# A fused attention and feed-forward block: where attention's steps are let into the matmul stream

## The chip, the cores and the metric

The kernel runs on one core of a Trainium2 chip. A core has a matrix engine (PE, TensorE), a vector engine (DVE), a scalar engine (ACT), a general engine (POOL, GpSimd) and a synchronising engine (SP); each works through its own queue in the order in which the program gave it the instructions, and waits there for semaphores of the others. DMAs are issued from the queues of SP, ACT and POOL. The metric is the device time of one execution in microseconds. Before the change the median of three runs is 1107.38 us (1107.1 to 1107.52).

## The reference

All tensors are float32; S = 2048 positions, D = 576, F = 4608, 32 heads of 18.

```python
x = A_x
xn = layernorm(x)                                  # no scale, no shift
q, k, v = split(xn @ wqkv)                         # 32 heads of 18
idx = pos[:, None] - 2 * arange(8)[None, :]        # 8 keys: this position, 2, 4, ... 14 before it
logits = einsum("bhsd,bhswd->bhsw", q, k[idx]) * 18 ** -0.5   # idx < 0: -1e9
o = einsum("bhsw,bhswd->bhsd", softmax(logits), v[idx])
attn = o @ wo
h = relu(xn @ w1 + b1); ffn = (h * h) @ w2 + b2
out = x + attn + ffn
```

The result is returned as [1, 2048, 576].

## The kernel before

**Tiling.** The positions are four blocks b of 512 (`TB`), worked on in two pairs, s = 0 (blocks 0, 1) and s = 1 (blocks 2, 3). float32 precision is had from two parts of every operand: a high part (an ACT copy into a type that PE takes fast) and a remainder (a DVE subtraction); each product is high by high, high by remainder and remainder by high, 128x128 weights against 512 positions. FFN1 of two blocks and two tiles of hidden units is one 2x2 block product, done with seven products instead of eight (slots T1, T3, B11, T2, B22, B21, T4; the sums of X are S1 to S3). What does not fit the 128-row grid (the last 64 rows of D) is a "left" product; in s = 1, from pair 2 on, it is replaced by one more matmul per product against a *stack* (`ST`, `LW`).

**Phases, in PE's order.** Layer norm and QKV of block 0; QKV of block 1 (`q0`); phase A of s = 0: 18 FFN1 pairs of block 0 and 1 with FFN2 of block 0 interleaved (`ffn_pair`, `work`); FFN2 of block 1 (`phase_b0`), while DVE and ACT normalise blocks 2 and 3; QKV of blocks 2 and 3 as four *halves* (k, half) of 14 quad steps each (`quads`, `quad_step`), the last two steps of which stand inside pair 0 of s = 1; phase A of s = 1; FFN2 of block 3 (`phase_b1`).

**An FFN1 pair** (line 605 on). PE: B11 into bank `ba`, T1 into `bc`, FFN2 work, T2 into `bb`, work, T3 into `bb`, B21 into `ba`, work, B22 into `bc`, T4 into `bb`, work. Between products ACT and DVE must free the banks: ACT copies `bb` to `u[:, 0]` after T2 (line 691) and to `u[:, 1]` after T3 (line 723), DVE adds `bc` to it (`r1[:, 1]`, line 725, recorded at the helper line 108), which is what B22 into `bc` waits for; later DVE adds `r0[:, 1]`, ACT does the `relu`s and squares. `splits` makes the high parts and remainders of the next weights: `w2_hi` (509), `w2_lo`, `w1_hi` (477), `left_weight_hi` (595). In pair 1 of s = 1 the stacks are built too: `stack_hi` on ACT, `stack_lo` on DVE, from the left rows `LR["a"]`.

**Attention runs beside PE.** Keys, values and queries are written by the QKV rows to memory (`kvq`) through a staging tile `st` of four places and loaded back per block and head group by POOL. `attention(b, g)` is a generator of 18 steps: four times a product of q and k (`qk`) and a reduction, a maximum with a subtraction that yields "exp", the exponential (ACT, line 396) with its sum, reciprocal and product, and four times a product with v (`pv`) and three halving sums. `statistics(b)` has four steps. `side(k, exp)` takes k steps of whatever is at the head of the queue; with `exp=False` it stops in front of an exponential. The places at which `side` is called, and with which k, are written out by hand: at the head of a pair, in its third product, at its end, in a table of quad steps, in the chunks of the output projection, between the tiles of FFN2. A step's K and V are loaded as soon as one of three `kv` tiles is given back. `complete(b)` runs whatever is still due before a block's attention output is gathered (`regroup`).

**QKV rows of blocks 2 and 3.** Each half produces eight rows (`row`, line 1047): an ACT copy of a bank into a place of `st` (line 1050), for every second one a DVE sum on top, and a store of 216 KB to `kvq` (line 1054) issued by ACT or SP. A place is used again four rows later. The tile `w1r` has two slots, used in turn for raw weights, left rows, stacks and left weights.

Of the kernel before, what the change touches and what calls it, by code (L numbers as in the profile page):

```python
# [8 lines left out]
F32 = mybir.dt.float32  # L9
# [7 lines left out]
P = 128  # L17
# [4 lines left out]
NJ = TB // P  # L22
# [6 lines left out]
QW = 3 * CG  # L29
# [10 lines left out]
T1, T3, B11, T2, B22, B21, LEFT, T4 = range(8)  # L40
# [5 lines left out]
def block_kernel(ctx: ExitStack, tc: tile.TileContext, x, xt, wqkv, wo, w1, b1, w2, b2, w1l, out):  # L46
# [3 lines left out]
    sb = ctx.enter_context(tc.tile_pool(name="sb", bufs=1))  # L50
# [24 lines left out]
    half = const.tile([P, 1], F32, name="half")  # L75
# [31 lines left out]
    def tt(out, a, b, op):  # L107
        return nc.vector.tensor_tensor(out=out, in0=a, in1=b, op=op)  # L108
# [204 lines left out]
    qp, stage = {}, {}  # L313
# [105 lines left out]
    current = [None, None, None]  # L419

    def side(k, exp=True):

        while k > 0:
            if current[0] is None:
                if not queue or queue[0][0] not in landed:
                    return k
                name, make = queue.pop(0)
                current[:] = [make(), None, name]
            if current[1] == "exp" and not exp:
                return k  # L430
            try:
                current[1] = next(current[0])
                k -= 1
            except StopIteration:
                current[0] = None
        return 0
# [38 lines left out]
    def w1_hi(n, k):  # L475
        w1s[n, k] = mt.tile([P, 2, 4, 2 * P], F32R, name="w1s", bufs=3)
        nc.scalar.activation(w1s[n, k][:, 0], raw1[n][:, 4 * k:4 * k + 4], AF.Copy)  # L477
# [33 lines left out]
    def w2_lo():  # L511
        i = los[0]
        los[0] += 1
        if i >= len(stream):
            return
        w = w2s[stream[i]]
        tt(w[:, DE:], raw2.pop(i)[:, :D], w[:, :D].bitcast(F32), ALU.subtract)
        load_w2(i + 3)
# [25 lines left out]
    ST, LW, LR = {}, {}, {}  # L544
# [16 lines left out]
    def stack_hi(to, v):  # L561
        nc.scalar.activation(to, v, AF.Copy)

    def stack_lo(to, v):
        rows = slice(L, 2 * L)
        tt(to[rows], v[rows], to[rows].bitcast(F32), ALU.subtract)
# [27 lines left out]
    def left_weight_hi(p):  # L594
        nc.scalar.activation(LW[p % 2], LR["w"], AF.Copy)

    def left_weight_lo(p):
        rows = slice(2 * L, P)
        tt(LW[p % 2][rows], LR["w"][rows], LW[p % 2][rows].bitcast(F32), ALU.subtract)
        load_left_weights(p + 1)  # L600
# [4 lines left out]
    def ffn_pair(s, p, work, first=False):  # L605
        b0, b1 = 2 * s, 2 * s + 1
        n = s * NP + p
# [73 lines left out]
            stack_hi(LR["st"][:, 0:2], LR["a"][:, 0:2])  # L681
            stack_hi(ST[T4], LR["a"][:, 3])
        if not first:
            side(1 if p == 1 else 3 if s else 2 + p % 2, s == 1)
        work(0)
        product(bb, T2, ss(2))
        own_w2 = first and s == 1
# [10 lines left out]
        def splits():  # L698
            if not own_w2:
                w2_lo()  # L700
            if not last and not s:
                w1_hi(n + 1, 0)
            if ready:
                left_weight_hi(p + 1)
            if s and p == 1:
                stack_lo(LR["st"][:, 0:2], LR["a"][:, 0:2])
                stack_lo(ST[T4], LR["a"][:, 3])
                stack_hi(ST[T1], LR["s"][:, 0])
            if not own_w2:
                w2_hi()  # L710
            if not last and not s:
                w1_lo(n + 1, 0)
            if ready:
                left_weight_lo(p + 1)
            if not own_w2:
                w2_lo()

        if not first:
            splits()
# [3 lines left out]
        nc.scalar.activation(u[:, 1], bb, AF.Copy)  # L723
        r0, r1 = four(), four()
        tt(r1[:, 1], bc, u[:, 1], ALU.add)
        if first:
            splits()
        if not last and s:
# [298 lines left out]
    rows_out = [0]  # L1027

    def quad_step(k, s, j, i):
        b0, b1, gs = 2, 3, (2 * k, 2 * k + 1)  # L1030
        a, b, c, u = [bank(n)[:, :QW] if opened is None else opened for n, opened in
                      zip((*QKV_BANKS[i], i), quad_banks[i])]
        quad_banks[i] = [a, b, c, u]
        js = slice(j * P, (j + 1) * P)

        def product(to, name, v, start=False):
            mm = [(v(0, n), ws[name][0][:, n]) for n in range(2)]
            for n in range(2):
                mm += [(v(0, n), ws[name][1][:, n]), (v(1, n), ws[name][0][:, n])]
            for n, (l, r) in enumerate(mm):  # L1040
                nc.tensor.matmul(to, l[:, js], r, start=start and n == 0, stop=n == len(mm) - 1, skip_group_check=True)  # L1041

        def left(to, f, v):
            for n in range(2):
                nc.tensor.matmul(to, v[:, js], ws[LEFT, f][:, n], start=False, stop=n == 1, skip_group_check=True)  # L1045

        def row(n, f, x, y=None):
            st = stage[0][:, rows_out[0] % NJ]
            rows_out[0] += 1
            nc.scalar.activation(st, x, AF.Copy)  # L1050
            if y is not None:
                tt(st, y, st, ALU.add)
            to = kvq[gs[f]][:, PAD + n * TB:PAD + (n + 1) * TB].rearrange("i (p j) c -> p j i c", j=NJ)[:, j]
            (nc.sync if y is not None else nc.scalar).dma_start(to, st.rearrange("p (i c) -> p i c", c=CG))

        ss = lambda n: lambda h, q: SS[n][:, h, q]
        if s == 1:
            product(a, B11, lambda h, q: X[b0][:, h, q], start=True)
            nc.scalar.activation(b, a, AF.Copy)
        if s == 2:  # L1060
            product(c, T1, ss(1), start=True)
        if s == 3:
            product(b, T2, ss(2))
            nc.scalar.activation(u, b, AF.Copy)
        if s == 4:
            left(c, 1, x4[b1])
            product(b, T3, ss(3))
            row(b1, 1, b, c)
        if s == 5:
            product(a, B21, lambda h, q: X[b0][:, h, 2 + q])  # L1070
            left(a, 0, x4[b0])
            row(b0, 0, a)
        if s == 6:
            product(c, B22, lambda h, q: X[b1][:, h, q])
            left(c, 1, x4["d"])
            row(b0, 1, c, u)
        if s == 7:
            product(b, T4, lambda h, q: X[b1][:, h, 2 + q])
            left(b, 0, x4[b1])
            row(b1, 0, b)  # L1080
# [3 lines left out]
    def phase_b0():  # L1084
# [41 lines left out]
        def hook(k, half, s, i):  # L1126
# [9 lines left out]
            if half and not k:  # L1136
# [32 lines left out]
                if (s, i) == (6, 1):  # L1169
# [3 lines left out]
                    for g in (0, 1):  # L1173
                        offer(2, g)
            if half and k:
                if (s, i) == (2, 1):
                    w1_again(NP, 0, nc.sync)
                if (s, i) == (5, 1):
                    complete(1)
                if (s, i) == (4, 1):  # L1180
                    w1_again(NP, 1, nc.sync)
# [5 lines left out]
        def quads(k, half, some):  # L1187
            for n in some:
                s, i = steps[n]
                quad_step(k, s, 2 * half + i, i)  # L1190
                if n in ((2, 3, 4, 8, 10, 12), (3, 6, 10, 12), range(1, 13), (3, 6, 8, 10))[2 * k + half]:
                    side(1)
                hook(k, half, s, i)

# [426 lines left out]
```

## Time and profile before

| | |
|---|---|
| median of three runs | 1107.38 us |
| profiled execution | 1107.93 us |
| its span, first to last instruction | 1106.2 us |
| PE busy / weight loads busy | 1096.8 / 925.2 us |
| DVE busy | 912.0 us |
| ACT busy | 575.0 us |
| POOL busy | 115.4 us |
| moved by DMA | 287.83 MB, mean 260 GB/s |
| granted clock of TensorE | 1.000 |

The page gives busy times by engine and by groups of instructions. A row of the waits reads: engine, line, what it waited for, us in total, how often, longest. A row of the order of time reads: start, duration, engine, line, operation, output<-input, shape, count, and in brackets the idle time before it with what ended it. Matmuls are pipelined: a 128x512 matmul is recorded with about 389 ns, and the next one starts before it ends, so the distance of starts is what to compare. SPq, ACTq, POOLq are the queues' own instructions, DMA issues among them.

### The profile page before, as it was taken

The numbers are of one execution on the slowest core, as the hardware profiler recorded it, in microseconds if no ns is written. First come the engines' busy times: TensorE is split into PE (matmuls) and PEld (weight loads), VectorE is DVE, ScalarE is ACT, GpSimd is POOL, SyncE is SP. The second block draws the span as 40 slices with busy tenths as digits, with TensorE's granted clock in tenths as the row PEclk, the third lists the DMA queues.
The fourth block names the chain that finished last, engine by engine and source line by source line (L and its number), as shares of the span: only waits on it lengthen the run. The fifth ranks groups of instructions, "written<-read, shape, count | busy, mean of one in ns | idle before, by whom it ended". The sixth has DMA issues, their size and how long they took to land.

```text
span 1106.2 us, 13892 instructions
## 1 busy us (share of the span) xinstructions
PE 1096.8 (99%) x4950; PEld 925.2 (84%) x4950; DVE 912.0 (82%) x1223; ACT 575.0 (52%) x809; POOL 115.4 (10%) x219
## 2 busy tenths in 40 slices
PE   9999999999999999999999999999999999999998
PEld 7998888888888888888899887888888888888887
DVE  7696979897996979999979488978988789899654
ACT  5435666556566654455344355555555555533342
POOL 4000101020020100100010200202102021000100
PEclk9999999999999999999999999999999999999999
DMA  8956987889699686866755887768686785866752
GB/s 297 329 177 234 333 309 255 296 214 372 229 244 392 220 357 214 311 247 226 259 164 169 309 263 300 259 260 308 238 315 240 267 314 205 316 208 205 280 193 81
DMA packets 100279, 287.83 MB, mean 260 GB/s; under 512 B 13288, under 2 KB 41712, under 8 KB 85488
## 3 DMA queue, kind: packets, MB, share of 16 engines
q1 hardware_dynamic: 65280, 188.15, 49.1%
q0 software_dynamic: 10544, 52.14, 12.9%
q10 hardware_dynamic: 24384, 46.64, 12.6%
q8 instruction: 39, 0.64, 0.2%
q14 instruction: 32, 0.26, 0.1%
HBM read 205.14 MB, written 81.74 MB: 259 GB/s over the span
## 4 chain that ended last, share of the span: by engine, by line
PE 89%; DVE 5%; DMA 3%; ACT 1%; issue 1%; ACTq 0%; POOL 0%; DVEq 0%; POOLq 0%; SPq 0%
PE p L536 46%; PE p L629 31%; PE p L1041 5%; PE p L635 3%; DMA kvq<-st 2%; PE p L338 1%; PE p L1401 1%; PE p L1045 1%; DVE pr L108 1%; DMA kv<-kvq 1%; DVE lg L387 1%; DVE w1r L108 1%; DVE r L108 0%; PE p L1318 0%; DVE h L108 0%
## 5 line engine op out<-in xcount | busy, mean ns | idle before, releaser
L536 PE MATMUL p<-h,w2s 128*128 128x512 f32 x2066 | 491.4, 389 | 0.1
L536 PEld LDWEIGHTS p<-h,w2s 128*128 128x128 f32 x2066 | 387.5, 188 | 81.5 <-ACT h L642 0.6
L629 PE MATMUL p<-X,w1s 128*128 128x512 f32 x864 | 219.7, 389 | 1.2 <-DVE r L108 0.9
L629 PEld LDWEIGHTS p<-X,w1s 128*128 128x128 f32 x864 | 162.0, 188 | 35.6 <-DVE r L108 1.3
L509 ACT ACTIVATE w2s<-w2r 128x640 fp32r<-128x640 f32 x164 | 120.2, 735 | 116.1 <-PE p L536 87.6
L629 PE MATMUL p<-S,w1s 128*128 128x512 f32 x648 | 164.8, 390 | 1.5 <-ACT r L691 1.5
L108 DVE TENSOR_TENSOR w2s<-w2r,w2s 128x576 fp32r<-128x576 f32 x164 | 123.4, 753 | 40.6 <-ACT w2s L509 39.8
L629 PEld LDWEIGHTS p<-S,w1s 128*128 128x128 f32 x648 | 121.4, 188 | 27.4 <-ACT r L691 2.3
L415 POOL DMA_DIRECT2D o<-q x128 | 69.2, 605 | 584.8 <-DVE q L108 582.8
L638 ACT ACTIVATE r<-r,b1t 128x512 f32<-128x512 f32 x72 | 52.0, 723 | 126.9 <-DVE r L108 125.2
L387 DVE TENSOR_REDUCE lg<-pr 128x64 f32<-128x1152 f32 x64 | 86.5, 1352 | 1.5
L108 DVE TENSOR_TENSOR pr<-lg,kv 128x1152 f32<-128x1152 f32 x64 | 86.7, 1354 | 1.3
L108 DVE TENSOR_TENSOR pr<-q,kv 128x1152 f32<-128x1152 f32 x64 | 86.6, 1353 | 0.8
L108 DVE TENSOR_TENSOR pr<-pr 128x576 f32<-128x576 f32 (+1 forms) x128 | 77.5, 605 | 3.2
L646 ACT ACTIVATE r<-r 128x1024 f32<-128x1024 f32 x72 | 76.1, 1057 | 1.2
L108 DVE TENSOR_TENSOR h<-r,h 128x1024 fp32r<-128x1024 f32 (+3 forms) x46 | 51.8, 1136 | 27.0 <-ACT r L646 18.8
L108 DVE TENSOR_TENSOR r<-p,r 128x512 f32<-128x512 f32 (+1 forms) x77 | 52.9, 688 | 20.3 <-PE p L629 9.8
L108 DVE TENSOR_TENSOR w1s<-w1r,w1s 128x1024 fp32r<-128x1024 f32 (+1 forms) x42 | 50.3, 1198 | 16.5 <-ACT w1s L477 16.4
L691 ACT ACTIVATE r<-p 128x512 f32<-128x512 f32 x36 | 21.5, 597 | 70.9 <-PE p L629 70.5
L638 ACT ACTIVATE r<-p,b1t 128x512 f32<-128x512 f32 x72 | 48.3, 672 | 0.0
L108 DVE TENSOR_TENSOR h<-h 128x1024 fp32r<-128x1024 f32 x36 | 43.9, 1220 | 4.8 <-ACT h L938 4.6
L536 PE MATMUL p<-w1s,w2s 128*128 128x512 f32 x195 | 44.7, 389 | 0.0
(193 smaller groups left out, 1174.2 us busy)
## 6 DMA issues: line engine op xcount, KB each, us to landing
w2r<-in_w SPq DMA_DIRECT2D x144, 320.0 KB, 3.4
kv<-kvq POOLq DMA_DIRECT2D x29, 1296.0 KB, 9.4
w<-w1s SPq DMA_DIRECT2D x36, 1024.0 KB, 8.4
w1s<-w ACTq DMA_DIRECT2D x34, 1024.0 KB, 7.3
h<-r SPq DMA_DIRECT2D x36, 512.0 KB, 6.3
h<-h SPq DMA_DIRECT2D x36, 512.0 KB, 4.2
w1r<-in_w SPq DMA_DIRECT2D x18, 640.0 KB, 7.7
kvq<-st ACTq DMA_DIRECT2D x48, 216.0 KB, 3.2
```

Of the source, the lines that this page charges most:

```text
L108: return nc.vector.tensor_tensor(out=out, in0=a, in1=b, op=op)
L338: nc.tensor.matmul(p[:, :QW], l, r, start=k == 0, stop=k == len(mm) - 1)
L387: nc.vector.tensor_reduce(out=lg[:, j * HG:(j + 1) * HG].rearrange("p a w -> p w a"), in_=pr.rearrange("p w (a d) -> p w a d", d=DH), axis ...
L415: nc.gpsimd.dma_start(rows[:, i], q[i * L:(i + 1) * L, :, a:z])
L509: nc.scalar.activation(w2s[stream[i]][:, :DE], raw2[i], AF.Copy)
L536: nc.tensor.matmul(yp[b][c], v, a, start=c not in yb[b], stop=c in last and c not in [o[0] for o in ops[i + 1:]], skip_group_check=True)
L629: nc.tensor.matmul(to, l, r, start=start and i == 0, stop=i == len(mm) - 1, skip_group_check=True)
L635: nc.tensor.matmul(to, weight(LEFT, k, f), v, start=False, stop=k == 1, skip_group_check=True)
L638: nc.scalar.activation(to, a, AF.Relu, bias=b1t[:, f:f + 1])
L646: nc.scalar.activation(r, r, AF.Square)
L691: nc.scalar.activation(u[:, 0], bb, AF.Copy)
L1041: nc.tensor.matmul(to, l[:, js], r, start=start and n == 0, stop=n == len(mm) - 1, skip_group_check=True)
```

## The change

There are four edits.

- `side` remembers at its start whether the generator stood at "exp" already when the call began (`pending`). If so, the exponential may be the first step of a call even with `exp=False`. An exponential reached within the call still stops it.
- The call at the head of a pair always has `exp=False`, and its k is changed. For s = 0 from 2 in even and 3 in odd pairs to 2, and 3 in every fourth (3, 7, 11, 15); for s = 1 from 3 to 2 in even and 3 in odd pairs. Pair 1 keeps 1. The table of the last QKV half calls `side` after steps 3 and 6 instead of 3, 6, 8 and 10.
- In pair 1 of s = 1 the two first `stack_lo` calls move from `splits` to a place behind the sum `r1[:, 1]`.
- In the last QKV half a second staging tile is opened in a slot of `w1r`; the first four rows of that half go to the first tile, the other four to the second.

```diff
     def side(k, exp=True):
 
+        pending = current[1] == "exp"
         while k > 0:
...
-            if current[1] == "exp" and not exp:
+            if current[1] == "exp" and not exp and not pending:
                 return k
+            pending = False
             try:
                 current[1] = next(current[0])
                 k -= 1
...
         if not first:
-            side(1 if p == 1 else 3 if s else 2 + p % 2, s == 1)
+            side(1 if p == 1 else 2 + (p % 4 == 3 if not s else p % 2), False)
         work(0)
...
             if s and p == 1:
-                stack_lo(LR["st"][:, 0:2], LR["a"][:, 0:2])
-                stack_lo(ST[T4], LR["a"][:, 3])
                 stack_hi(ST[T1], LR["s"][:, 0])
...
         tt(r1[:, 1], bc, u[:, 1], ALU.add)
+        if s and p == 1:
+            stack_lo(LR["st"][:, 0:2], LR["a"][:, 0:2])
+            stack_lo(ST[T4], LR["a"][:, 3])
         if first:
             splits()
...
         def row(n, f, x, y=None):
-            st = stage[0][:, rows_out[0] % NJ]
+            st = stage[rows_out[0] // NJ % len(stage)][:, rows_out[0] % NJ]
...
             if half and k:
+                if (s, i) == (1, 0):
+                    stage[1] = sb.tile([P, NJ, QW], F32, name="w1r", bufs=2)
                 if (s, i) == (2, 1):
                     w1_again(NP, 0, nc.sync)
...
-                if n in ((2, 3, 4, 8, 10, 12), (3, 6, 10, 12), range(1, 13), (3, 6, 8, 10))[2 * k + half]:
+                if n in ((2, 3, 4, 8, 10, 12), (3, 6, 10, 12), range(1, 13), (3, 6))[2 * k + half]:
                     side(1)
```

## The prediction

> **What bounds the kernel now.** I read the page's first part, then the waits of PE alone, then the order of time around each wait.
>
> ```profile
> span 1106.2 us, 13892 instructions
> PE 1096.8 (99%) x4950; PEld 925.2 (84%) x4950; DVE 912.0 (82%) x1223; ACT 575.0 (52%) x809; POOL 115.4 (10%) x219
> ```
>
> ```profile
> PE p L1318 <- DVE lg L1311: 2.1, 1, 2.1
> PE p L629 <- ACT r L691: 1.5, 2, 0.8
> PE p L629 <- DVE r L108: 0.9, 1, 0.9
> ```
>
> PE is the bound. The first wait is the kernel's start, which the change does not touch; the other two rows are three single stalls in FFN1's second half (line 629 is `product`). The most that an edit of ACT's, DVE's or SP's order can bring is the sum of these stalls. The order of time of PE shows them:
>
> ```profile
> 625.89 0.55 PE L1045 MATMUL p<-r,x 128*128 128x432 f32 x2
> 626.28 1.52 PE L629 MATMUL p<-S,w1s 128*128 128x512 f32 x6
> ...
> 628.82 0.55 PE L1045 MATMUL p<-r,x4d 128*128 128x432 f32 x2
> 630.21 1.65 PE L629 MATMUL p<-S,w1s 128*128 128x512 f32 x6 [0.85 <-ACT r L691]
> 631.70 0.70 PE L635 MATMUL p<-x,w1s 128*128 128x512 f32 x2
> ...
> 658.58 1.75 PE L536 MATMUL p<-h,w2s 128*128 128x512 f32 x7
> 660.17 1.52 PE L629 MATMUL p<-S,w1s 128*128 128x512 f32 x6
> 661.53 1.52 PE L629 MATMUL p<-X,w1s 128*128 128x512 f32 x6
> ...
> 663.34 1.75 PE L536 MATMUL p<-h,w2s 128*128 128x512 f32 x7
> 666.02 1.65 PE L629 MATMUL p<-X,w1s 128*128 128x512 f32 x6 [0.93 <-DVE r L108]
> 667.51 0.62 PE L635 MATMUL p<-x4d,w1s 128*128 128x512 f32 x2
> ...
> 677.71 1.75 PE L536 MATMUL p<-h,w2s 128*128 128x512 f32 x7
> 680.16 1.66 PE L629 MATMUL p<-S,w1s 128*128 128x512 f32 x6 [0.70 <-ACT r L691]
> ```
>
> Matmuls overlap, so starts are compared, not idle time. Undisturbed, two matmuls of line 1045 are followed after 0.39 (625.89 to 626.28), a block of seven after 1.59 (658.58 to 660.17), six of `product` after 1.36 (660.17 to 661.53). Stall 1: 630.21 - 628.82 - 0.39 = 1.00 us; stall 2: 666.02 - 663.34 - 1.59 = 1.09; stall 3: 680.16 - 677.71 - 1.59 = 0.86. The first six matmuls after a stall take 1.49 instead of 1.36 (630.21 to 631.70, 666.02 to 667.51), 0.13 more each. Together 1.00 + 1.09 + 0.86 + 3 x 0.13 = 3.34 us, 0.30% of the time. That is the ceiling of this change.
>
> A measurement of this kernel can tell about 0.2% (2.2 us) from no change; so nearly the whole ceiling must be reached for a visible gain.
>
> **The change part by part.**
>
> ```profile
> 628.59 0.53 ACT L1050 ACTIVATE st<-p 128x432 f32<-128x432 f32 x1 [4.46 <-DMA kvq<-st]
> ...
> 678.58 0.42 ACT L396 ACTIVATE lg<-lg 128x256 f32<-128x256 f32 x1 [1.74 <-DVE lg L108]
> ...
> 679.53 0.58 ACT L691 ACTIVATE r<-p 128x512 f32<-128x512 f32 x1
> ```
>
> ```profile
> 662.64 1.82 DVE L108 TENSOR_TENSOR w1r<-w1r 32x1024 fp32r<-32x1024 f32 x2
> 664.48 0.76 DVE L108 TENSOR_TENSOR w2s<-w2r,w2s 128x576 fp32r<-128x576 f32 x1
> 665.27 0.69 DVE L108 TENSOR_TENSOR r<-p,r 128x512 f32<-128x512 f32 x1
> ...
> 684.18 0.68 DVE L108 TENSOR_TENSOR r<-p,r 128x512 f32<-128x512 f32 x1
> ```
>
> *Eight places (stall 1).* Row 7 of the last QKV half goes into a place of `st` whose earlier content is still on its way to memory; ACT stands 4.46 us (628.59) with the bank copy of line 691 behind it, for which PE stops. With rows 5 to 8 in a second tile none of them waits for a store of its own half, and the copy follows T2 at once: -1.13 (1.00 and its restart). The new tile takes a slot of `w1r`, whose two raw weight tiles were read for the last time at the end of the second half; `open_stacks` takes the slot over in pair 1, behind the five chunks of the output projection, when its stores have long landed. So the slot costs nothing. But one thing stands right behind this stall:
>
> ```profile
> PEld p L635 <- DMA w1s<-w: 0.2, 1, 0.2
> w1s<-w SPq DMA_DIRECT2D x1, 1024.0 KB, 11.1
> 616.93 0.77 POOL L360 DMA_DIRECT2D kv<-kvq  x1
> kv<-kvq POOLq DMA_DIRECT2D x29, 1296.0 KB, 9.4
> kv<-o POOLq DMA_DIRECT2D x1, 768.0 KB, 8.9
> ```
>
> The weights of line 635, issued on SP behind a row store, land after 11.1 us; PE took them at 631.70 with 0.2 of waiting. Without stall 1 it wants them 1.0 earlier. They are slow because POOL's V load (616.93, 1296 KB) and the output gather behind it (768 KB and a smaller part) run at the same time: about 3.1 MB in 11.1 us, 0.28 MB/us. By the count of steps below, V load and gather go out some 12 us earlier, while a K load of 1296 KB, which before waited for a step in pair 1, comes forward to about 612. All three should be nearly through when the weights are issued: if only the 768 KB are out of the way, the weights land 2.7 us earlier (an estimate from these rows), and 1.0 is needed. I take the cost as nothing; its bounds are nothing and the whole 1.13.
>
> *Remainders after the sum (stall 2).* The two `stack_lo` (1.82 us) stood ahead of the sum `r1` at 665.27 for which PE waits. Now the second `w2s` remainder can start at 662.64 (0.76) and the sum at 663.4, done at 664.1, while PE arrives at 663.34 + 1.59 = 664.93. Margin 0.8: -1.09 and the restart, -1.22. The 1.82 is only moved, to 664.1 until 665.9, where DVE stood at the end of the sum before (665.27 + 0.69). Behind it wait `left_weight_hi` on ACT, whose tile reuses the slot of `LR["a"]`, and through it DVE's own weight remainder; both come after the `relu` of the sum, which is now 1.8 earlier, so the wait for the pair is covered. The stacks are first multiplied in pair 2.
>
> *Exponential (stall 3).* Pair 2 takes max, exponential and a product at its head; ACT waits 1.74 for DVE's subtraction, and line 691 comes only at 679.53. By the count below, attention (2,0) now has its exponential in pair 0, between FFN2's chunks, and pair 2 begins with a sum and a product. Line 691 then runs as soon as T2 is done: -0.86 and the restart, -0.99. What is late next: `r1` of pair 2.
>
> ```profile
> 685.05 1.54 PE L629 MATMUL p<-X,w1s 128*128 128x512 f32 x6
> ```
>
> Before, `r1` ended at 684.86, 0.19 before PE wanted the bank (685.05). PE now comes 0.86 + 1.09 = 1.95 earlier; DVE gains 1.09 with PE, and max, exponential and product give way to sum and product, which saves the maximum and DVE's wait for ACT, an estimated 1.0. The margin stays about 0.2: I take +0.1, bounds 0 and +0.5.
>
> *The number of steps.* Counted by hand through `side`. FFN1's first half (s = 0): pairs 2 to 17 asked for 8 x 2 + 8 x 3 = 40 leading steps and all calls together lost 15 steps standing at "exp"; now they ask for 12 x 2 + 4 x 3 = 36 and lose 3, at the ends of pairs 2, 5 and 15. So 40 - 15 = 25 become 33: eight more are done, and all that follows comes eight steps earlier. Attention (1,0), which ended in the last half, ends at the sixth step of the half before. In s = 1 pairs 2 to 17 ask for 40 instead of 48, and with the losses at "exp" and the two steps taken from the last half the end of all attention moves from tile 16 to tile 20 of the last phase, ten tiles before its output is wanted (tile 30). Every K and V load is still issued at least a pair ahead of its step, in program order on the same queues; no step should wait for data.
>
> Eight added steps in the first half: DVE must hide them.
>
> ```profile
> 153.30 1.23 DVE L108 TENSOR_TENSOR w1s<-w1r,w1s 128x1024 fp32r<-128x1024 f32 x1 [2.86 <-ACT w1s L477]
> ...
> 155.75 0.69 DVE L108 TENSOR_TENSOR r<-p,r 128x512 f32<-128x512 f32 x1 [0.46 <-ACT r L723]
> ```
>
> ```profile
> 158.32 1.52 PE L629 MATMUL p<-X,w1s 128*128 128x512 f32 x6
> ```
>
> This is pair 3, whose head was empty and gets three steps: exponential, product and sum, at most 1.35 + 2.90 = 4.3 us by the rows below. DVE idles 2.86 + 0.46 ahead of `r1`, and `r1` ends 158.32 - 155.75 - 0.69 = 1.88 before PE needs its bank: 5.2 of room. I cost these steps at nothing; the cover left is 0.9.
>
> The shifted steps in the QKV halves are the one place without room:
>
> ```profile
> 590.69 1.35 DVE L108 TENSOR_TENSOR pr<-q,kv 128x1152 f32<-128x1152 f32 x1
> ...
> 598.80 0.60 DVE L108 TENSOR_TENSOR st<-p,st 128x432 f32<-128x432 f32 x1
> 599.31 1.35 DVE L108 TENSOR_TENSOR pr<-lg,kv 128x1152 f32<-128x1152 f32 x1
> 600.69 1.25 DVE L108 TENSOR_TENSOR pr<-pr 128x576 f32<-128x576 f32 x2
> ...
> 602.21 0.60 DVE L108 TENSOR_TENSOR st<-p,st 128x432 f32<-128x432 f32 x1
> ```
>
> ```profile
> 600.61 1.33 PE L1041 MATMUL p<-h,X 128*128 128x432 f32 x6
> ```
>
> In the third half DVE is behind. Six steps stand ahead of row (4,0)'s sum: 8.11 us (590.69 to 598.80); PE writes that bank again at 600.61, 1.21 after the sum's end. Now these six are three pairs of product and sums, 2.90 each (599.31 to 602.21): 8.70, +0.59. The half before ends on a sum instead of a reduction (+0.2) and has the exponential behind ACT's row copy: DVE's wait there lies between 0 and the 1.74 that the engines cost each other at 678.58; I take 0.5, nearer to nothing, since both queues come there at about the same time. So 0.59 + 0.2 + 0.5 = 1.3 against 1.21: a new stall of 0.1 plus 0.13 of restart, and 0.2 at the next such row. Cost +0.4, bounds 0 and 1.7.
>
> Sum: -1.13 - 1.22 - 0.99 + 0.1 + 0.4 = -2.84. The profiled execution took 1107.93 (span 1106.2 and 1.7 around it), 0.55 more than the median; it would be 1105.1, the median 1107.38 - 2.84 = **1104.5**.
>
> A rule bears on the ceiling. The Trainium skill, Perfetto Trace Analysis, section Identifying the Most-Contended Engine, calls matmul busy time a poor measure of the distance to the limit and takes the weight loads' share instead. That share is 84% here, so by it PE would have 16% of reserve and could make up a stall of 1 us. By that rule the sum would be 0 and the time 1107.4; by the rows it is -2.84. The trace does not agree with the rule here: after a stall six matmuls take 1.49 and later ones the usual 1.36, and nothing is made up.
>
> **Rivals.**
> - *Forecast*: three stalls gone, 0 to 1 us given back: 1104.1 to 1105.2. Chance 0.57.
> - *The weights come no earlier.* PE stops at line 635 until 631.70 whatever ACT does: stall 1 stays under another name, 1104.5 + 1.13 = 1105.6. For it: the 11.1 and the 0.2. Against: the V load and the gather move. Decides if landing stays over 10.2. Chance 0.14.
> - *DVE too late in the third half and in pair 2*: 1.7 and 0.5 instead of 0.4 and 0.1: 1106.2. For it: 1.21 of room against 1.3. Chance 0.12.
> - *PE has reserve and makes up its stalls.* Weight loads fill 84% of the span; were the rest free, 3.34 us would be caught up within some 20 us and the time stays 1107.4. Against: the pace after the stalls in the rows above. Chance 0.05. It is what the rule of the Trainium skill's page Perfetto Trace Analysis, cited above, would make of it.
> - *Slower: the first half's DVE does not hide the eight steps.* The exponential at a pair's head makes DVE wait for ACT, which squares and copies a bank first; place: ahead of `r1` in pairs 3, 6, 13 and 16 and in the fuller pairs between. Price: 8 steps at 1.35 = 10.8 if nothing is hidden, 1115.3; it decides against the change from 2.84 on, a quarter of that, and visibly from 5.0: 1109.6. Against it: 5.2 of room beside 4.3. Chance 0.12.
>
> **How the numbers follow.** Faster by over 0.2% means under 1105.17: nearly all of the forecast (0.55) and a part of the third rival (0.05): 0.60. Within 0.2%: the rest of the forecast, the weights, most of the late DVE, the reserve: 0.28. Slower: 0.12. The range reaches from the ceiling with a little noise (1103.8) to 1107.4, where no change ends; outside lie the slower case and some hundredths below. The forecast's own range is 1103.9 to 1105.3.
>
> **What would show it.** Right: PE's waits list has neither row of line 629 from the second half; ACT's row copies in the last half show no wait for the store; `r1` of pair 1 starts before the two 32-partition remainders; line 396 is not in pair 2. Given back: a PE stall of line 1041 behind DVE's row sum near 600.6. Wrong: line 635 waiting for its weights near 631; PE waits behind DVE between 140 and 410; the load of the weights still at 11 us.

## The result and the profile after

The changed kernel takes 1110.87 us (median of 6 runs, 1110.31 to 1112.76), the kernel before 1107.26 beside it (6 runs): ratio 1.0035 [1.0023, 1.0048]. It is 0.35% slower; the forecast was 0.26% faster. The profiled execution took 1110.40 with a span of 1108.7.

After the change, the page's first part and the waits of PE alone. Line numbers moved: `product` is now line 631, its short products line 637, FFN2 538, the QKV products 1044 and 1048, the row copy 1053.

```profile
span 1108.7 us, 13885 instructions
PE 1097.4 (99%) x4950; PEld 924.4 (83%) x4950; DVE 911.3 (82%) x1223; ACT 574.6 (52%) x809; POOL 116.2 (10%) x219
```

```profile
PE p L1323 <- DVE lg L1316: 2.1, 1, 2.1
PE p L631 <- DMA w1s<-w: 1.9, 1, 1.9
PE p L1044 <- ACT st L1053: 1.2, 2, 0.8
PE p L538 <- DVE w2s L108: 1.0, 1, 1.0
PE p L538 <- DVE S L921: 0.6, 1, 0.6
```

Both rows of FFN1's second half that made up the ceiling (line 629 behind ACT's copy and behind DVE's sum) are gone. Four other rows have come, five stalls in all. In the order of time of PE, the three old places first:

```profile
634.05 0.55 PE L1048 MATMUL p<-r,x4d 128*128 128x432 f32 x2
634.44 1.52 PE L631 MATMUL p<-S,w1s 128*128 128x512 f32 x6
...
667.30 1.75 PE L538 MATMUL p<-h,w2s 128*128 128x512 f32 x7
668.89 1.52 PE L631 MATMUL p<-X,w1s 128*128 128x512 f32 x6
...
680.45 1.75 PE L538 MATMUL p<-h,w2s 128*128 128x512 f32 x7
682.04 1.52 PE L631 MATMUL p<-S,w1s 128*128 128x512 f32 x6
```

The starts follow each other at the undisturbed 0.39, 1.59 and 1.59 us: all three stalls are gone. And the new ones:

```profile
545.16 2.57 PE L538 MATMUL p<-h,w2s 128*128 128x512 f32 x10 [0.98 <-DVE w2s L108]
...
581.06 1.43 PE L1044 MATMUL p<-h,X 128*128 128x432 f32 x6 [0.43 <-ACT st L1053]
...
621.55 1.43 PE L1044 MATMUL p<-h,X 128*128 128x432 f32 x6 [0.80 <-ACT st L1053]
...
626.89 1.63 PE L631 MATMUL p<-X,w1s 128*128 128x512 f32 x6 [1.94 <-DMA w1s<-w]
...
975.92 2.33 PE L538 MATMUL p<-h,w2s 128*128 128x512 f32 x9 [0.57 <-DVE S L921]
```

PE runs the same 4950 matmuls in the same order in both kernels. So the time can be booked matmul by matmul: the start of each one in a kernel's trace minus the start of the same one in the trace before, and where this difference changes, time was lost (+) or won (-). This is worked out from the rows of the order of time. In us, by the times of the trace before, from 100 us on. What lies ahead of that is left out: at the kernel's start and at a stall near 93 us the traces of all kernels of this document differ by up to 1.1 us, though they run the same instructions there.

```
stretch   what runs there                        after - before
100-460   FFN1 first half, FFN2 block 1 begins      -0.20
460-530   FFN2 block 1, middle                      +0.52
530-560   FFN2 block 1, end                         +1.79
560-610   second and third QKV half                 +0.95
610-629   last QKV half, pair 0 begins              +3.27
629-640   stall 1                                   -1.27
640-672   stall 2                                   -1.22
672-690   stall 3                                   -1.02
690-940   FFN1 second half                           0.00
940-1000  its end, FFN2 block 3 begins              +0.85
1000-end                                             0.00
sum                                                 +3.67
```

The sum is near the medians' 1110.87 - 1107.26 = 3.61; it books one execution of each kernel, so that it comes so near is in part luck. The change did what it was said to do, -3.51, and paid 7.18 elsewhere, 6.5 of it between 460 and 629, a part of the kernel in which none of the three stalls lay.

**Where the 6.5 us come from.** But for a part of the +1.79 (see the ledger of all kernels below), the runs below put it down to the eight attention steps that are done earlier. Three ways can be read in the traces. First, DVE at the end of FFN2's block 1, before the change:

```profile
528.00:536.00 8.00, 8.00 (x37) 6.64 (x36) 7.93 (x9) 2.15 (x3) 0.54 (x1) 1.00 0.50 159
536.00:544.00 8.00, 8.00 (x37) 6.64 (x36) 7.31 (x13) 4.29 (x6) 0.00 (x0) 1.00 0.94 365
```

```profile
542.97 1.42 DVE L108 TENSOR_TENSOR w2s<-w2r,w2s 128x576 fp32r<-128x576 f32 x2
```

and after it (the length of a stretch, busy time of PE, weight load, DVE, ACT and POOL in it, then the granted clock, the DMA share and GB/s; then DVE's order):

```profile
536.00:544.00 8.00, 7.91 (x34) 5.80 (x32) 7.83 (x11) 2.37 (x4) 3.71 (x8) 1.00 0.65 242
```

```profile
541.70 1.35 DVE L108 TENSOR_TENSOR pr<-q,kv 128x1152 f32<-128x1152 f32 x1
543.09 1.35 DVE L387 TENSOR_REDUCE lg<-pr 128x64 f32<-128x1152 f32 x1
544.36 1.42 DVE L108 TENSOR_TENSOR w2s<-w2r,w2s 128x576 fp32r<-128x576 f32 x2
```

Tiles 29 to 32 used to hold two products with their reductions, a maximum, an exponential and one pair of product and sums; now they hold three such pairs and one product with its reduction, and DVE, which already was at 7.3 to 7.9 of 8, has nothing left. The pair of `w2s` remainders behind them begins at 544.36 instead of 542.97, and PE waits 0.98 for the first.

Second, the exponential of the next attention comes into a QKV half, behind a row copy on ACT and ahead of the next row copies. DVE waits 1.39 for it, so DVE's next subtraction for `w1r` is late, ACT's split of that weight waits 2.30 for the subtraction, and the row copies stand behind the split. PE, which needs their bank, stops at 581.06 (0.70 in the ledger). ACT's and DVE's rows after the change:

```profile
576.94 0.42 ACT L396 ACTIVATE lg<-lg 128x256 f32<-128x256 f32 x1 [0.44 <-ACT st L1053]
...
579.66 0.93 ACT L977 ACTIVATE w1s<-w1r 128x864 fp32r<-128x864 f32 x1 [2.30 <-DVE w1r L108]
580.50 0.93 ACT L1053 ACTIVATE st<-p 128x432 f32<-128x432 f32 x2
```

```profile
577.39 0.42 DVE L397 TENSOR_REDUCE sm<-lg 128x32 f32<-128x256 f32 x1 [1.39 <-ACT lg L396]
```

Third, and largest, POOL's transfers. After the change the store of the attention output, the V load, the two parts of the output gather, and a K load with its q go out between 602 and 614:

```profile
602.17 4.33 POOL L415 DMA_DIRECT2D o<-q  x8 [14.98 <-DVE q L108]
606.29 0.75 POOL L360 DMA_DIRECT2D kv<-kvq  x1
608.00 0.54 POOL L848 DMA_DIRECT2D kv<-o  x1 [0.95 <-DMA o<-q]
611.06 0.54 POOL L848 DMA_DIRECT2D kv<-o  x1 [2.52 <-issue]
611.59 0.54 POOL L358 DMA_DIRECT2D q<-kvq  x1
613.45 0.54 POOL L360 DMA_DIRECT2D kv<-kvq  x1 [1.32 <-DVE pr L108]
```

This is the moment at which SP loads the first weights of pair 0 (slots 0 to 3, 1 MB); ACT's rows show what the row stores do. SP's order, the landing of that load alone, ACT's order and the stretches, all after:

```profile
612.38 0.76 SPq L489 DMA_DIRECT2D w1s<-w  x1
```

```profile
w1s<-w SPq DMA_DIRECT2D x1, 1024.0 KB, 14.5
```

```profile
620.97 0.95 ACT L1053 ACTIVATE st<-p 128x432 f32<-128x432 f32 x2 [4.35 <-DMA kvq<-st]
...
624.39 0.53 ACT L1053 ACTIVATE st<-p 128x432 f32<-128x432 f32 x1 [2.47 <-DMA kvq<-st]
```

```profile
612.00:616.00 4.00, 4.00 (x22) 3.85 (x21) 2.51 (x2) 1.03 (x2) 0.67 (x2) 1.00 1.01 365
616.00:620.00 4.00, 4.00 (x22) 3.85 (x21) 0.00 (x0) 0.53 (x1) 0.00 (x0) 1.00 1.05 427
```

Before, the same load was issued at 610.24, ahead of POOL's burst (616.93), and landed in 5.0:

```profile
610.24 0.33 SPq L487 DMA_DIRECT2D w1s<-w  x1
```

```profile
w1s<-w SPq DMA_DIRECT2D x1, 1024.0 KB, 5.0
```

Now the load shares the DMA engines with the burst, at 365 to 427 GB/s, and takes 14.5; PE waits 1.94 for it at 626.89. The row stores beside it are late too, and since the first four rows of the last half still go into the four old places, ACT waits 4.35 and 2.47, and PE 0.80 at 621.55. The Trainium skill says of this, in DMA: Bandwidth & Descriptors, section Issuing engines are not separate DMA queues, that transfers run on the same 16 DMA engines whichever engine issued them and interleave there; the trace agrees (5.0 against 14.5 us).

The 0.85 near 976 has its own root. ACT's split of an FFN2 weight waits for the load there (after):

```profile
969.96 0.74 ACT L511 ACTIVATE w2s<-w2r 128x640 fp32r<-128x640 f32 x1 [5.48 <-DMA w2r<-in_wo]
```

The split is late, so DVE's drains are, and PE waits 0.57 for a drain. Why that load is late stays open: no run moved it, and `e3_late_loads` below, whose attention steps stand in the same places from there on, loses nothing here.

### The profile page after: what moved, and what is told of

Read it like the earlier page. It is cut to its first block, busy times and chain, and to the rows that moved or that the text cites. A ratio compares the mean times of both kernels' runs of the same rounds, so it can differ in the third digit from the quotient of the medians.

```text
span 1108.7 us, 13885 instructions
## 1 busy us (share of the span) xinstructions
PE 1097.4 (99%) x4950; PEld 924.4 (83%) x4950; DVE 911.3 (82%) x1223; ACT 574.6 (52%) x809; POOL 116.2 (10%) x219
## 3 DMA queue, kind: packets, MB, share of 16 engines
q10 hardware_dynamic: 24384, 46.64, 12.5%
## 4 chain that ended last, share of the span: by engine, by line
PE 89%; DVE 5%; DMA 3%; issue 1%; ACT 1%; ACTq 0%; POOL 0%; SPq 0%; DVEq 0%; POOLq 0%
PE p L538 43%; PE p L631 32%; PE p L338 7%; PE p L637 3%; PE p L1044 2%; DVE pr L108 2%; DMA w1s<-w 1%; DMA kvq<-st 1%; DVE w2s L108 1%; PE p L1406 1%; DMA w2r<-in_w 1%; DVE w1s L108 1%; PE p L1048 0%; DVE r L108 0%; DVE h L108 0%
## 5 line engine op out<-in xcount | busy, mean ns | idle before, releaser
L108 DVE TENSOR_TENSOR r<-p,r 128x512 f32<-128x512 f32 (+1 forms) x77 | 53.0, 688 | 18.9 <-ACT r L723 11.6
L360 POOL DMA_DIRECT2D kv<-kvq x29 | 16.4, 565 | 270.8 <-DVE pr L108 129.4
```

## The experiments

Theory after the result: the three edits to the second half do what was forecast; the eight early steps cost the rest, through DVE at the end of block 1 and through the time at which loads and stores meet. Rivals: the second tile of places is itself at fault (stores into it, its slot); or the second half's fewer steps are. The ledger of all (stretches as above, same unit; the sum includes 100-460 and 690-940, which are not shown: -0.23 to +0.05 in the one, nothing in the other but +0.29 in `e4_skip8`):

```
                    460-530 530-560 560-610 610-629 629-640 640-672 672-690 940-1000 1000-end   sum
after                 +0.52   +1.79   +0.95   +3.27   -1.27   -1.22   -1.02    +0.85     0.00  +3.67
e1_stack               0.00   +0.47    0.00    0.00    0.00   -1.22   -0.01    -0.01     0.00  -0.76
e2_places              0.00    0.00    0.00    0.00   -0.13    0.00   -0.03    -0.01     0.00  -0.17
e3_late_loads         +1.32   +1.80   +1.66   +0.03   -1.27   +0.45   -0.60    -0.01    +0.03  +3.19
e4_skip8              +1.27    0.00    0.00    0.00   -0.37   -1.22   -0.96    +0.81    +0.53  +0.13
e6_old_first           0.00   +0.80    0.00   +0.03   -0.07   -1.22   -1.02    +0.79    +0.40  -0.27
e7_old_first_v         0.00   +0.53    0.00    0.00   +0.49   -1.22   -1.02    +0.79     0.00  -0.38
e8_places_v            0.00   +1.20    0.00   +0.04   +2.75    0.00    0.00    +0.01     0.00  +4.03
e9_first_only         +1.90   +1.79   +0.96   +4.23   -1.27   +0.52   +0.34    -0.01     0.00  +8.25
e10_all_v              0.00   +1.23    0.00   +0.03   -1.27   -1.22   -1.02    +0.80    +1.19  -0.27
e11_places_stack_v    +0.10   +1.17   +0.01   +0.04   -1.27   -1.22   -0.02    -0.01     0.00  -1.21
e12_pair2              0.00   +0.63    0.00    0.00   -1.27   -1.22   -1.02    -0.01     0.00  -2.89
```

The column 530-560 lies between 0 and 1.23 in kernels that take the steps there as the kernel before does, and at 1.79 or 1.80 in the three that take them eight steps early; the trace before is among the lowest, so a part of the +1.79 is the spread of that place between executions. So is 460-530 no fixed price: the four kernels with the early steps run the same program up to there and lose 0.52 to 1.90. A row books one execution and can lie up to 3 us off the difference of the medians (`e7_old_first_v`: -0.38 against +2.48, its profiled execution being the fastest of twelve).

**One part alone: the remainders** (`e1_stack`: kernel before, `stack_lo` moved)

```diff
             if s and p == 1:
-                stack_lo(LR["st"][:, 0:2], LR["a"][:, 0:2])
-                stack_lo(ST[T4], LR["a"][:, 3])
                 stack_hi(ST[T1], LR["s"][:, 0])
...
         tt(r1[:, 1], bc, u[:, 1], ALU.add)
+        if s and p == 1:
+            stack_lo(LR["st"][:, 0:2], LR["a"][:, 0:2])
+            stack_lo(ST[T4], LR["a"][:, 3])
```

> The kernel before with one edit alone: the two stack_lo calls of pair 1 (s = 1) behind the sum r1. If the reading of stall 2 holds, the stall at 666.02 goes and nothing takes its place: 1107.3 - 1.2 = 1106.1 us, with stalls 1 and 3 where they were. Rival: DVE is as late at the next sum (r0), the stall only moves one product on: 1107.3.

Measured: 1106.5 us against 1107.84, ratio 0.9987 [0.9978, 0.9996]. Stall 2 is gone, -1.22, and nothing takes its place. In the ledger this part is worth what was forecast to the hundredth; by the medians it is 1.34.

**One part alone: the eight places** (`e2_places`: kernel before)

```diff
-            st = stage[0][:, rows_out[0] % NJ]
+            st = stage[rows_out[0] // NJ % len(stage)][:, rows_out[0] % NJ]
...
+                if (s, i) == (1, 0):
+                    stage[1] = sb.tile([P, NJ, QW], F32, name="w1r", bufs=2)
```

> The kernel before with one edit alone: eight places for the staged rows of the last QKV half. Attention's loads stay where they were. If the weights of line 635 bind behind the stall, the stall leaves T3 (630.21) and PE waits at line 635 until 631.7 instead: 1107.1. If they do not bind: 1106.1. If the second tile itself is what makes the rows late in the changed kernel (its stalls at 621.55 and 626.89): 1108.5 or more.

Measured: 1108.08, ratio 1.0003 [0.9994, 1.0012]. A row from PE's waits:

```profile
PE p L635 <- DMA w1s<-w: 0.9, 1, 0.9
```

T3 begins 1.1 earlier and line 635 then waits 0.9 for its weights, which land when they did before. By itself this part wins 0.13. Alone it also costs nothing, so the rival "the second tile is at fault" falls.

**The burst, moved** (`e3_late_loads`: changed kernel, the V load of attention (2,0) and the q and K loads of (2,1) issued on SP in pair 0)

```diff
+            late = (kind, b, g) in (("v", 2, 0), ("k", 2, 1))
+            issue = held.append if late else lambda f: f(lane[0])
...
                 load_left_weights(2)
+                for f in held:
+                    f(nc.sync)
+                held.clear()
```

> The changed kernel, every step in its place, but the V load of attention (2,0) and the K and q load of (2,1) are issued on SP in pair 0 of s = 1 instead of on POOL at about 606 and 612. Theory A (these loads, pulled forward by eight steps, run against the row stores and the first weights of pair 0): the stalls at 621.55 and 626.89 go, 1110.9 - 3.2 = 1107.7. Theory B (DVE, loaded otherwise, is late everywhere): no change, 1110.9.

Measured: 1110.19, ratio 1.002 [1.0011, 1.0029]. The 1107.7 of theory A was missed, and so was theory B. 610-629 falls from +3.27 to +0.03: PE's wait of 1.94 for the first weights is gone, and they land in 7.2 us instead of 14.5, so the delay was the work of these loads (POOL's gather stays where it is). The stall behind the row stores is not: 0.71 of it now stands earlier, in the column 560-610, where ACT waits 4.24 for a place. And 640-672 goes from -1.22 to +0.45: behind 2.9 MB on SP the splits of h and w2 for FFN2 in pairs 0 and 1 come late (ACT waits 4.49 for a load there). Moved like this, the transfers in the main change whom they hold up.

**The steps, taken out of block 1's end** (`e4_skip8`: changed kernel, no steps in tiles 29 to 32, so that the QKV halves take the steps that they took before)

```diff
-                    run(pieces, 2 if n > 21 else 1 + n % 2)
+                    run(pieces, 2 if n > 21 else 1 + n % 2, n < 29)
```

> The changed kernel without the eight attention steps at the end of FFN2 of block 1 (its tiles 29 to 32), so that from the QKV halves on every step stands where it stood before the change. If the eight steps gained in the first half are the cause of all new stalls from 475 to 627, those go (1.7 + 0.4 at 475 to 545, 0.6 and 0.25 in the halves, 3.2 at 621 and 627) and stalls 2 and 3 stay away: 1104.7 to 1105.6, the upper end if the weights of line 635 bind again near 631.7. If the cause is another edit: 1109 or more.

Measured: 1108.11, ratio 1.0001 [0.9992, 1.001]. That is 2.5 us over the range that was expected, but everything between 530 and 629 is gone. What is left in the first part is 460-530. It was read from the traces, and no run moved the load alone: a V load that waited until 534.65 before now goes out at 453.79, between FFN2's own loads (also after the change, where ACT waits 5.00 for `w2r` instead of 4.18), and stall 1 moves to the weights as in the kernel with the places alone. Later 0.29, 0.81 and 0.53 are lost; the 0.81 is the stall shown with the next run, the causes of the others stay open.

**The first half as before** (`e6_old_first`: changed kernel)

```diff
-        pending = current[1] == "exp"
+        pending = current[1] == "exp" and second[0]
...
-            side(1 if p == 1 else 2 + (p % 4 == 3 if not s else p % 2), False)
+            side(1 if p == 1 else 2 + p % 2, False)
...
     def phase_a(s, filler):
         b = 2 * s
+        second[0] = s == 1
```

> The changed kernel, with FFN1's first half asking for its steps as before the change (40 leading steps, 15 of them lost at "exp"), so that the eight steps are not taken early; eight places, the remainders behind the sum and the new step rules of the second half stay. Theory (the eight early steps are the cause of every new stall): the five stalls of 538 to 627 us are gone (together 5.7 us), as is the +0.4 of 467 to 496; stalls 2 and 3 stay gone, stall 1 only changes its name to line 635: 1.0 to 1.2 + 0.9 to 1.0 = 2 us under the kernel before, ratio 0.997 to 0.9985. Rival 1 (part of the loss belongs to the second tile or to the second half's new step counts): a stall of 0.5 us or more is left between 538 and 627 or ahead of 976, ratio 0.999 to 1.001. Rival 2 (without the early steps the exponential stands at the head of pair 2 or of another pair again): stall 3 comes back in the FFN1 half, ratio about 0.999.

Measured: 1108.06 (11 runs, 1106.03 to 1110.29), ratio 0.9997 [0.9989, 1.0006]. 460-530 and 560-629 are at nothing, and 530-560 is within its spread, so the early steps were the cause. But the time is no better than before, and the 0.997 to 0.9985 of the theory was missed: line 635 waits 0.91, and 1.2 us go at 940 and later, much as the second rival had it. Here the exponential stands at the head of one of the last pairs. DVE's row, and PE's behind it:

```profile
944.76 0.42 DVE L397 TENSOR_REDUCE sm<-lg 128x32 f32<-128x256 f32 x1 [1.67 <-ACT lg L396]
```

```profile
949.93 6.28 PE L540 MATMUL p<-h,w2s 128*128 128x512 f32 x25 [0.26 <-ACT h L646]
```

That is stall 3's pattern in another pair: the new step rule of the second half moves it. The four kernels that have that rule and no steps taken early in the halves lose 0.8 at this place, and none without the rule does. In the two with the rule and the early steps the exponential stands elsewhere: the changed kernel loses its 0.85 by the late weight load, `e3_late_loads` nothing.

**The early steps alone** (`e9_first_only`: kernel before)

```diff
-            side(1 if p == 1 else 3 if s else 2 + p % 2, s == 1)
+            side(1 if p == 1 else 3 if s else 2 + (p % 4 == 3), s == 1)
...
+        pending = current[1] == "exp" and not second[0]
...
-            if current[1] == "exp" and not exp:
+            if current[1] == "exp" and not exp and not pending:
                 return k
+            pending = False
```

> The kernel before, with FFN1's first half alone asking for its steps as in the change (36 leading steps, one pending exponential let through, eight more steps done by its end); four places, remainders ahead of the sum and second half as before. Theory (the eight early steps cost what the changed kernel lost): the stalls of 538 to 627 us appear here too, +4 to +6 us by 627; stall 2 stays; stall 3 may go, since its exponential comes earlier; 1110.5 to 1113.5, ratio 1.003 to 1.0055. Rival (the stalls come from the steps together with the second tile of places or the fewer steps of the last half): less than 2 us by 627, ratio 1.000 to 1.0015.

Measured: 1115.54, ratio 1.0067 [1.0055, 1.008]: more than expected. 8.9 us are lost between 460 and 629, by the same stalls. With four places in the last half it is 4.23 there instead of 3.27, mostly by one stall more, at 630.86 (0.76), where ACT waits 2.21 for a place; the number of places is not the only difference of the two kernels, so that the second tile saves this in the changed kernel was not shown.

**The V load beside line 635's weights** (`e7_old_first_v` on the kernel with the old first half, `e8_places_v` on the kernel before with the places; the V load is issued on POOL, at its place in pair 0)

```diff
+            held.append(load) if (kind, b, g) == ("v", 2, 0) else load()
...
                 load_left_weights(2)
+                held.pop()()
```

> The kernel of the row above, and POOL's V load of attention (2,0) (1296 KB) is issued in pair 0 of FFN1's second half and no more ahead of the output gather. Theory (line 635's weights are slow because V load and gather run beside them): the weights land within 8 us instead of 11, PE stops neither at T3 nor at line 635, all three stalls are gone, some 3.2 us under the kernel before, ratio 0.9965 to 0.9975. Rival (the weights are slow by their own place behind row stores on SP): line 635 still waits 0.7 to 1, ratio as in the row above. Second rival (the load moved into pair 0 delays the h, w2 and left-row loads there): a new stall of 0.5 to 1.5 between 640 and 670, ratio 0.998 to 0.999.

> The kernel before with the eight places and with the V load of attention (2,0) issued in pair 0 of FFN1's second half; nothing else. With the eight places alone stall 1 went from T3 to line 635 and the time stayed (ratio 1.0003). Theory (V load and gather hold the weights up): landing falls from 11 to at most 8 us, line 635 does not wait, 1.0 to 1.1 us under the kernel before, ratio 0.999. Rival (they are slow for another reason): landing stays at 10 to 12, ratio 1.000.

Measured: 1110.32, ratio 1.0019 [1.0009, 1.003], and 1110.41, ratio 1.0017 [1.0008, 1.0027]: both expectations missed. A later place in the program is not a later issue on an engine that has nothing else to do. POOL's order, the landing, and PE's order in the second kernel:

```profile
620.33 0.53 POOL L362 DMA_DIRECT2D kv<-kvq  x1 [0.48 <-issue]
```

```profile
w1s<-w SPq DMA_DIRECT2D x1, 1024.0 KB, 12.5
```

```profile
633.26 1.22 PE L638 MATMUL p<-x,w1s 128*128 128x512 f32 x2 [2.24 <-DMA w1s<-w]
```

The V load went out at 620.33 instead of 616.93, only behind the gather; so more of it lay beside the weights (issued at 620.76), which took 12.5 instead of 11.1 (11.6 in the first kernel). The overlap grew instead of shrinking and the weights came later, which speaks for the same cause.

**The V load after the weights** (`e10_all_v` on the changed kernel with the old first half, `e11_places_stack_v` on the kernel before with places and remainders; V on SP at the end of pair 0)

```diff
                 nc.sync.dma_start(kept(b, NC - 1), yleft)
+                held.pop()(nc.sync)
```

> The changed kernel with FFN1's first half asking for its steps as before, and the V load of attention (2,0) put on SP behind the rows, weights and left rows, at the end of pair 0. (Put on POOL in pair 0, it was issued at 620.1 to 620.3 whatever its place in the program, since POOL had nothing else to do, and the weights then came 1 to 2 us later.) Theory (V load beside the weights of line 635 holds them up): the load is issued after 643, the weights land within 9 us, line 635 waits less than 0.2; all three stalls gone, PE 3.2 us ahead of the kernel before at 690. Of this 0.6 to 0.8 is given back near 951, where the exponential now stands at the head of a pair: 2.4 to 3.2 us faster, ratio 0.997 to 0.998. Rival (gather and row stores alone keep the weights at 11): line 635 waits 0.9 again, ratio 0.998 to 0.9995. Second rival (on SP it delays pair 0's h, w2 or drains): a new stall between 645 and 670 of 0.5 to 1.5.

> The kernel before with the eight places, the remainders behind the sum and the V load of attention (2,0) on SP at the end of pair 0; the steps of both halves as before. Theory: stalls 1 and 2 gone, stall 3 stays, nothing at 951: PE 2.2 us ahead from 666 on until the end, ratio 0.998. Rival (weights bound by other transfers): 1.1 to 1.3, ratio 0.999. If PE loses 0.6 near 951 here too, the loss there isn't due to the second half's step rule.

Measured: 1106.63, ratio 0.9987 [0.9978, 0.9996], and 1105.15, ratio 0.9974 [0.9965, 0.9984]. The weights land in 9.6 us in the first and 8.5 in the second, line 635 waits in neither, and no transfer on SP is in the way at 640 to 672. The first has all three stalls gone, but not the 0.997 to 0.998 of its theory: it gives 0.80 back near 950, again by the second half's step rule, and 1.19 behind 1000, of it 0.71 where ACT waits 6.54 for a load of an FFN2 weight. That the rule causes the latter was not shown: `e7_old_first_v` has the same rule and loses nothing there. The second has stalls 1 and 2 gone as expected, keeps the old rule and gives nothing back near 950.

**Stall 3 without that rule** (`e12_pair2`: the last kernel, and pair 2's head alone may not take an exponential)

```diff
-            side(1 if p == 1 else 3 if s else 2 + p % 2, s == 1)
+            side(1 if p == 1 else 3 if s else 2 + p % 2, s == 1 and p != 2)
```

> The kernel of the row above, and the exponential isn't let through at the head of pair 2 alone (it comes with the third product of that pair); every other call asks for its steps as before. Theory (stall 3 is that one exponential's place): all three stalls gone, nothing at 951: 3.2 to 3.4 us faster, ratio 0.997. Rival (the third product's sum becomes late in pair 2, since two steps with the exponential stand ahead of it): a new stall of 0.5 to 1 at about 683, ratio 0.998.

Measured: **1104.26 us** (1103.43 to 1104.79), ratio 0.9966 [0.9954, 0.9979] to the kernel before (1107.98 beside it), as expected and the best of all. PE's waits, its order at stall 1's place, SP's order and the landing of line 635's weights:

```profile
PE p L1325 <- DVE lg L1318: 2.1, 1, 2.1
PE p L1045 <- DVE h L922: 0.2, 1, 0.2
PE p L539 <- ACT h L645: 0.2, 1, 0.2
```

```profile
629.51 1.52 PE L632 MATMUL p<-S,w1s 128*128 128x512 f32 x6
630.88 0.62 PE L638 MATMUL p<-x,w1s 128*128 128x512 f32 x2
```

```profile
643.89 0.45 SPq L362 DMA_DIRECT2D kv<-kvq  x1
```

```profile
w1s<-w SPq DMA_DIRECT2D x1, 1024.0 KB, 8.9
```

Beside the wait at the kernel's start no wait of PE is over 0.2. The whole gain of the three stalls is had without moving any of the eight steps.

## Why the prediction was wrong

- *The ceiling of 3.34 us, the pace after a stall:* right. Three stalls gone are -1.27 - 1.22 - 1.02 = -3.51. The rule of the Trainium skill that was weighed there (Perfetto Trace Analysis, Identifying the Most-Contended Engine) isn't borne out by any run: whatever PE lost or won by 690 stands to the hundredth at 940 in eleven kernels, and the twelfth (`e4_skip8`) loses 0.29 more on the way; none makes anything up.
- *Eight places, -1.13:* -1.27 in the changed kernel, though not for the reason given. "All three should be nearly through when the weights are issued": line 635's weights landed in 6.0 only because PE and the rows were 5 us late by then, and the load was issued at 626.05. With the old first half they take 11.1 and the gain is 0.07 to 0.13, which was the rival "the weights come no earlier".
- *Remainders, -1.22:* right, alone and together.
- *Exponential, -0.99, and r1 of pair 2, +0.1:* -1.02 and nothing. `r1` of pair 2 has little room, as was said: it loses 0.37 in `e3_late_loads` and 1.29 in `e9_first_only`. What the working missed is that the rule lets an exponential stand at other heads: it costs 0.8 at the end of the half in four other kernels (not in the changed one), and stall 3 is removed by one pair's condition without this.
- *The count of steps, eight more:* right as far as the traces show: V load and gather went out 10 us earlier (forecast 12) and the K load at 613.45 (forecast 612).
- *First half, cost nothing:* right. Between 100 and 460 the ledger has -0.20. The rival that had the kernel slower there did not happen.
- *Third QKV half, +0.4 (0 to 1.7):* 0.95 from 560 to 610. The stall behind DVE's row sum near 600.6 came as sized, 0.24 against 0.1 + 0.13. But DVE's wait for the exponential, taken as 0.5 between 0 and 1.74, is 1.39, and in the half before, where it falls, it stops PE at 581.06 by way of ACT's split and row copy. That path was not followed, and its 0.70 was not in the sum. The 0.2 at the next row did not come.
- *The step that failed* is the pair of sentences "The shifted steps in the QKV halves are the one place without room" and "no step should wait for data". The first: DVE at the end of block 1 was at 7.93 of 8 us in the trace before, and the eight steps pass through there as well; that was put at nothing and measured +1.79, with the spread named above. The second is true of the steps and left out everyone else: not they wait for the loads that come earlier, but weights, row stores and `w2` splits that run beside them. This too was put at nothing and measured +3.27 between 610 and 629, shown by moving the loads and by taking the steps out, and +0.52 between 460 and 530, where the load was not moved alone. The forecast looked at one transfer that the earlier burst might help (line 635's) and not at the one 10 us ahead of it, issued at 610.24, into which it moved.

With the forecast's gains and the measured losses the sum is -3.3 + 0.9 + 1.8 + 3.3 + 0.5 + 0.8 = +4.0, not -2.84. The two stretches of transfers, 3.3 and 0.5, are nearly all of it; without them it would be near nothing, and still not a gain.

## What to carry to other kernels

Work that is taken earlier takes its transfers along: for each load, store and gather that moves, list which other transfer of the same 10 us has someone waiting behind it, on every queue. Read the spare time of an engine in all stretches through which moved work passes, not only where it begins. And before a rule is changed for all iterations to cure one stall, try the condition for that one iteration: here it brought the gain without the cost.

## What the runs showed of the hardware

One stall cost more than its length. In the kernel before with the places and the V load on POOL, PE waited 2.24 us until 633.26 and then ran at half clock. The stretches there, in the order of numbers given above (the granted clock is the third number from the end):

```profile
631.20:633.26 2.06, 0.00 (x1) 0.00 (x1) 1.76 (x1) 0.46 (x1) 0.00 (x0) 0.95 1.05 431
633.26:636.60 3.34, 3.34 (x8) 2.66 (x9) 1.90 (x3) 0.72 (x1) 0.00 (x0) 0.52 1.05 385
636.60:638.00 1.40, 1.40 (x8) 1.14 (x7) 0.00 (x0) 0.65 (x2) 0.00 (x0) 1.00 1.03 408
```

Eight matmuls took 3.34 us at a mean clock of 0.52; undisturbed ones start every 0.23. In finer stretches the clock is 1.00 from 631.02, where PE's last matmul ended, to 633.04, and 0.50 from there to 636.46: it fell 2.02 us into the wait and stayed down for 3.42 us. The ledger has +2.75 there; the kernel with the old first half and V on POOL, whose clock stays at 1.00, waits 1.44 at the same place and books +0.49. After the 1.94 of the changed kernel the clock was still 1.00 in the profiled execution. The runs' mean clocks point the same way: of the 12 runs of the kernel with the old first half and V on POOL, the six at 0.999 or 1.0 took 1107.30 to 1110.03, the six at 0.996 to 0.998 took 1110.62 to 1112.46; and the two of the changed kernel's six at 0.998 took 1112.09 and 1112.76, the others 1110.31 to 1111.26. That in these runs it is the same stall was not shown, since only one execution of each was profiled. The Trainium skill (TensorE: Matmul & The Clock Gate, What's actually happening) has the clock halved after an idle window of about 3.4 us that runs freely; the length at half clock agrees, 3.42 us, but here 2.0 us of idle sufficed.
